# Moving the work tiles of an attention and MLP kernel by 32 bytes in SBUF, relative to the weights

## The chip, the cores and the metric

One core of one Trainium2 chip runs the whole program. The metric is the time of one execution in device microseconds; the time of a kernel is the median of its runs.

## What is computed

Attention with 4 sink positions and a sliding window of 128, over 4 batches of 8 heads of 768 tokens with head size 64, and then a two-layer MLP on the 3072 resulting rows.

```python
scores = scale * np.matmul(q, k.transpose(0, 1, 3, 2))
keep = is_sink | in_window
scores = np.where(keep, scores, -1000000000.0)
a = np.exp(scores - max); a = a / (np.sum(a, axis=-1, keepdims=True) + 1e-09)
x = np.matmul(a, v)            # heads side by side: (3072, 512)
h = x @ w_in                   # (512, 2048)
g = h * erf(softplus(h))
return g @ w_out               # (2048, 512)
```

## The kernel before

The MLP works on 12 groups of 256 tokens. For each group it goes over 16 blocks of 128 hidden columns (`hidden`, L524 to L535), and multiplies each pair of blocks with the second weights (`project`, L560 to L573). Attention for the next group is computed in between, in 48 steps of two heads each (`load`, `prep`, `core`, `norm`, `ptrans`, `av`, `xfin`), placed by a table `plan` and by priorities.

Apart from the first group, both products are made from values split in two parts of type float32r. The weights lie as `wt` tiles of two parts; the tokens as `xh` and `xl` (written in `xfin`); the hidden values as `g` with two parts (written in `act`). Three products of parts make one product:

- L533, `h<-xh,wt` and `h<-xl,wt`: a slice of `wt` of 128 x 128 is loaded into TensorE (PEld), then 256 columns of `xh` or `xl` are streamed through it (PE). 12 such pairs make one block of one group; 2112 in all.
- L570, `o<-wt,g`: 128 x 128 of `g` are loaded, then 512 columns of `wt` are streamed. 1056 in all.

So `x` streams against loaded `wt`, and `wt` streams against loaded `g`. While one matmul streams, the weight load of the next one runs. In the first group the same two products are made in plain fp32 instead (L529 and L570 with `wf`, `xf` and `gf`), as two passes of the matmul.

SBUF is given out by pools, one after another, in the order in which the pools are opened: `wpool` (33 tiles of 4096 bytes in each partition), then `pers` (`tri`, `kq`, `sv`, `pst`, two `sh` tiles and a tile `gap` that nothing reads or writes), then `raw` (the loaded `q`, `k`, `v`) and `work` (`u`, `pt`, `uo`, `sp`, `xh`, `xl`, `r`, `g`, `acc`). All `wpool` tiles have the same rest modulo 256, since 4096 is a multiple of 256; call it W. The tiles of `pers` take 64 + 11520 + 2048 + 4608 + 896 + 896 bytes, and `gap` another 128, together 20160 = 78 x 256 + 192. So `raw` and `work` begin at W + 192, that is 64 bytes below W modulo 256; every tile in them is a multiple of 256 bytes long, and so they all begin there. `kq`, `sv` and `pst` begin at W + 64, and `sh` at W + 64 and W + 192.

```python
shs = [pers.tile([P, 7, 2 * SW], F32R, name=f"sh{i}") for i in range(2)]
for x in shs:
    nc.gpsimd.memset(x[:, 6].bitcast(F32), 0.0)
pers.tile([P, 32], F32, name="gap")
```

With "distance" this document means the address of the operand that is being loaded as weights minus that of the operand that is being streamed at that time, modulo 256. Within L533 it is +64 before the change, and within L570 it is -64. At the change from a run of L533 to one of L570 (`g` loaded while `x` streams) it is 0, and so it is from L570 to L533.

Of the kernel before, what the change touches and what calls it, by code (L numbers as in the profile page):

```python
# [9 lines left out]
F32 = mybir.dt.float32  # L10
# [9 lines left out]
P = 128  # L20
# [30 lines left out]
def kernel(  # L51
# [77 lines left out]
    def fast_path():  # L129
        with ExitStack() as st:  # L130
            pers = st.enter_context(tc.tile_pool(name="pers", bufs=1))
# [44 lines left out]
            shs = [pers.tile([P, 7, 2 * SW], F32R, name=f"sh{i}") for i in range(2)]  # L176
            for x in shs:
                nc.gpsimd.memset(x[:, 6].bitcast(F32), 0.0)
            pers.tile([P, 32], F32, name="gap")
            xp = {}  # L180

            stp = {}
# [397 lines left out]
    def general_path():  # L580

        NT_S = S // P
        with ExitStack() as st:
# [71 lines left out]
            with tc.tile_pool(name="g_one1", bufs=1) as one, tc.tile_pool(name="g_work1", bufs=2) as work:  # L655
# [3 lines left out]
                with tc.For_i(0, B, 1) as b:  # L659
                    for gb in range(GPB):  # L660
# [25 lines left out]
                        for i in range(2):  # L686
# [3 lines left out]
                            )  # L690

    fast_path()
    ok = nc.values_load(flagi[0:1, 0:1], min_val=0, max_val=1)
    with tc.If(ok == 0):
# [31 lines left out]
```

## Time and profile before

| | |
|---|---|
| median of 3 runs | 765.98 us (763.82 to 767.38) |
| the profiled execution | 765.26 us |
| its span, first to last instruction | 763.3 us |
| TensorE matmul (PE) busy | 718.0 us, 94% |
| weight load (PEld) busy | 598.2 us, 78% |
| VectorE (DVE), ScalarE (ACT), GpSimd (POOL) busy | 69%, 70%, 27% |

Three views matter here. The busy time by stretch tells which engine is full, and at what clock. The groups by line tell how many matmuls there are of each kind; their mean is the length of one from its start to its end, which overlaps with the next one. The timeline merges equal instructions that follow each other, with the start of the first and a count: the start of a later row less that of an earlier one, divided by the number of matmuls between, is the time that one matmul takes of the engine, and is called its spacing here.

### The profile page before, as it was taken

Reading aid. Unit: us, or ns where it says so; the run is one execution under the profiler, and the core shown is the slowest. Engines: PE = TensorE matmul, PEld = TensorE weight load, DVE = VectorE, ACT = ScalarE, POOL = GpSimd, SP = SyncE. Lnnn points to the kernel's source line nnn. Section 1 sums busy time; section 2 is a strip of 40 time slices with the busy share of each in tenths; the row PEclk is TensorE's granted clock in tenths of the full one; section 3 lists DMA queues with packets and bytes.
Section 4 is the critical chain, followed back from the end, with each engine's and each line's share of the span. In section 5 each row is a group of like instructions: output and inputs, shape, how many; then the busy total and the mean of one; then the engine's idle time right before and its main releaser. Section 6 shows DMA issues by size and latency. Waiting matters only on the chain.

```text
span 763.3 us, 14942 instructions
## 1 busy us (share of the span) xinstructions
PE 718.0 (94%) x5168; PEld 598.2 (78%) x5168; DVE 526.5 (69%) x1509; ACT 535.0 (70%) x1261; POOL 202.6 (27%) x212
## 2 busy tenths in 40 slices
PE   2577998999999999999999999999999999999997
PEld 2345664887888898888888888888888888888885
DVE  6978998888676576576586586586576586584352
ACT  2356578897786687677787687687686687686473
POOL 1211220133322223232322232332322232322122
PEclk8679998999999999999999999999999999999999
DMA  6776530211211211211121211111111111100000
GB/s 203 218 231 198 218 86 15 76 23 26 61 44 31 67 45 25 63 31 32 56 49 30 59 42 37 55 41 29 56 38 42 56 46 36 39 12 1 28 1 32
DMA packets 100595, 47.33 MB, mean 62 GB/s; under 512 B 89248, under 2 KB 93344, under 8 KB 100512
## 3 DMA queue, kind: packets, MB, share of 16 engines
q1 hardware_dynamic: 100224, 46.29, 21.8%
q8 instruction: 43, 0.70, 0.4%
q14 instruction: 40, 0.33, 0.1%
q10 hardware_dynamic: 288, 0.00, 0.0%
HBM read 37.88 MB, written 6.29 MB: 58 GB/s over the span
## 4 chain that ended last, share of the span: by engine, by line
PE 76%; DVE 10%; ACT 6%; DMA 4%; issue 2%; SPq 1%; POOL 1%; ACTq 0%; DVEq 0%; POOLq 0%
PE o L570 30%; PE h L533 27%; PE av L361 5%; PE ps L272 4%; PE tqk L220 3%; PE tp L317 3%; PE h L529 2%; DVE pst L307 2%; DVE acc L552 1%; ACT u L550 1%; DMA ws<-in_moe_w_out_dram 1%; PE ts L338 1%; DVE w L442 1%; ACT pst L293 1%; DMA out_dram<-ot 1%
## 5 line engine op out<-in xcount | busy, mean ns | idle before, releaser
L570 PE MATMUL o<-wt,g 128*128 128x512 f32 x1056 | 270.0, 399 | 1.1 <-POOL g L558 0.5
L570 PEld LDWEIGHTS o<-wt,g 128*128 128x128 f32 x1056 | 189.0, 188 | 36.5 <-POOL g L558 1.3
L533 PE MATMUL h<-xh,wt 128*128 128x256 f32 x1408 | 203.7, 282 | 1.8 <-DVE acc L552 1.1
L533 PEld LDWEIGHTS h<-xh,wt 128*128 128x128 f32 x1408 | 184.7, 189 | 11.4 <-DVE acc L552 1.8
L558 POOL TENSOR_TENSOR g<-acc,g 128x512 fp32r<-128x512 f32 x88 | 114.7, 1303 | 291.7 <-DVE g L557 182.7
L550 ACT ACTIVATE u<-r 128x512 f32<-128x512 f32 x288 | 165.0, 623 | 13.5 <-DVE wf L448 4.4
L323 POOL TENSOR_SCALAR_AFFINE_SELECT uo<-pt 128x512 f32<-128x512 f32 (+1 forms) x96 | 83.1, 887 | 252.5 <-ACT pt L319 231.8
L552 DVE SCALAR_TENSOR_TENSOR acc<-u,acc 128x512 f32<-128x512 f32 x176 | 128.4, 730 | 19.1 <-ACT u L550 2.8
L552 DVE SCALAR_TENSOR_TENSOR acc<-u,h 128x512 f32<-128x512 f32 x88 | 60.4, 687 | 108.3 <-POOL g L558 60.3
L533 PE MATMUL h<-xl,wt 128*128 128x256 f32 x704 | 111.2, 279 | 0.0
L293 ACT ACTIVATE pst<-pst,kq 128x144 f32<-128x144 f32 x192 | 77.4, 405 | 25.7 <-DVE kq L289 24.6
L533 PEld LDWEIGHTS h<-xl,wt 128*128 128x128 f32 x704 | 94.2, 188 | 0.0
L545 ACT ACTIVATE r<-h 128x512 f32<-128x512 f32 x96 | 57.0, 593 | 25.8 <-PE h L533 24.9
L546 ACT ACTIVATE r<-r 128x512 f32<-128x512 f32 x96 | 61.1, 637 | 2.0
L547 ACT ACTIVATE r<-r 128x512 f32<-128x512 f32 x96 | 60.6, 631 | 2.6
L307 DVE TENSOR_SCALAR pst<-pst,kq 128x144 f32<-128x144 f32 x192 | 57.2, 360 | 1.5
L317 PE MATMUL tp<-ident,pst 128*128 128x128 f32 x192 | 36.4, 291 | 17.5 <-DVE pst L307 17.2
L557 DVE CAST g<-acc 128x512 fp32r<-128x512 f32 x88 | 44.3, 504 | 12.1 <-PE o L570 8.1
L223 ACT COPY kq<-tqk 128x512 f32<-128x512 f32 x48 | 28.0, 585 | 33.7 <-PE tqk L220 31.6
L361 PE MATMUL av<-uo,v 128*64 128x128 f32 (+1 forms) x512 | 50.1, 328 | 1.2 <-POOL uo L323 1.2
L377 ACT CAST xh<-av 128x256 fp32r<-128x256 f32 x44 | 16.0, 365 | 49.2 <-PE av L361 49.2
L272 PE MATMUL ps<-kq 64*64 64x208 f32 (+1 forms) x768 | 49.5, 369 | 0.0
(78 smaller groups left out, 723.0 us busy)
## 6 DMA issues: line engine op xcount, KB each, us to landing
ws<-in_moe_w_in_dram SPq DMA_DIRECT2D x16, 512.0 KB, 5.8
ws<-in_moe_w_out_dram SPq DMA_DIRECT2D x16, 512.0 KB, 5.0
q<-in_q_dram SPq DMA_DIRECT2D x96, 64.0 KB, 2.2
k<-in_k_dram SPq DMA_DIRECT2D x96, 64.0 KB, 2.2
v<-in_v_dram SPq DMA_DIRECT2D x64, 96.0 KB, 2.4
out_dram<-ot SPq DMA_DIRECT2D x24, 256.0 KB, 2.0
v<-in_v_dram SPq DMA_DIRECT2D x32, 64.0 KB, 2.2
kq<-kq SPq DMA_DIRECT2D x32, 64.0 KB, 2.0
```

The lines of the kernel that those rows point to most:

```text
L272: nc.tensor.matmul(ps[h][hf, x : x + n], qt[r, hf], kt[r, r0 : r0 + n], start=True, stop=True),
L293: nc.scalar.activation(y, y, AF.Exp, bias=d["neg"][:, i, h : h + 1], scale=-1.0, accum_out=d["sum"][:, i, h : h + 1])
L307: nc.vector.tensor_scalar_mul(p, p, sm[:, i, h : h + 1])
L323: nc.gpsimd.affine_select(out=uo[:, :, i1:, e, :], in_=pt[:, :, i1:, :], pattern=[[0, 2], [0, 2 - i1], [-sg, P]], compare_op=op, fill=0.0, ...
L361: prev, nc.tensor.matmul(o, x[:, h, :], y[:, h, :], start=False, stop=(m == len(ops) - 1), skip_group_check=True)
L533: nc.tensor.matmul(o, wt[NC * j + c][:, p, fs], xt[e][:, c, :], start=(m == 0), stop=(m == len(ops) - 1))
L546: nc.scalar.activation(r, r, AF.Square, bias=b_v, scale=-0.5)
L547: nc.scalar.activation(r, r, AF.Square, bias=b_r)
L550: nc.scalar.activation(u, r, AF.Square, bias=b_a[i], scale=CS)
L552: nc.vector.scalar_tensor_tensor(out=acc, in0=u, scalar=CC[i] * CS**2, in1=x, op0=ALU.add, op1=ALU.mult)
L558: nc.gpsimd.tensor_tensor(gl, acc, gh.bitcast(F32), op=ALU.subtract)
L570: nc.tensor.matmul(self.acc[g, i], gt[e][:, n0 : n0 + P], w, start=(f == 0 and m == 0), stop=(f == NF - 1 and m == len(ops) - 1),)
```

## The change

The unused tile `gap` grows from 32 to 40 floats, so every tile of `raw` and `work` moves up by 32 bytes in each partition. They begin 32 bytes below W modulo 256 now. The tiles of `wpool` and the other tiles of `pers` stay, and no instruction is added, removed or put elsewhere. The distance within L533 becomes +32, that within L570 -32; at the change from one to the other it stays 0.

```diff
             for x in shs:
                 nc.gpsimd.memset(x[:, 6].bitcast(F32), 0.0)
-            pers.tile([P, 32], F32, name="gap")
+            pers.tile([P, 40], F32, name="gap")
             xp = {}
```

## Rows read from the trace of the kernel before

**Rows 1.** The page, part 1: engine busy us (share of the span) and instructions.

```profile
PE 718.0 (94%) x5168; PEld 598.2 (78%) x5168; DVE 526.5 (69%) x1509; ACT 535.0 (70%) x1261; POOL 202.6 (27%) x212
```

**Rows 2.** Busy time by stretch: us, then each engine, clock, DMA share, GB/s.

```profile
0.00:50.00 50.00, 22.44 (x153) 14.64 (x153) 41.74 (x158) 17.33 (x60) 9.16 (x22) 0.75 0.75 226
50.00:100.00 50.00, 44.64 (x238) 31.29 (x236) 43.10 (x114) 28.89 (x71) 8.38 (x8) 0.94 0.62 200
...
200.00:300.00 100.00, 99.62 (x767) 85.95 (x767) 68.91 (x200) 77.01 (x180) 28.63 (x29) 1.00 0.19 47
...
600.00:700.00 100.00, 99.63 (x774) 86.64 (x772) 67.25 (x195) 75.91 (x176) 30.01 (x28) 1.00 0.13 34
700.00:763.30 63.30, 56.68 (x349) 49.57 (x345) 23.35 (x38) 34.50 (x59) 12.93 (x10) 1.00 0.05 19
```

**Rows 3.** Groups by line on PE: count, busy us, mean ns, idle before.

```profile
L570 PE MATMUL o<-wt,g 128*128 128x512 f32 x1056 | 270.0, 399 | 1.1 <-POOL g L558 0.5 <-ACT ot L577 0.4
L533 PE MATMUL h<-xh,wt 128*128 128x256 f32 x1408 | 203.7, 282 | 1.8 <-DVE acc L552 1.1 <-DVE gf L552 0.7
L533 PE MATMUL h<-xl,wt 128*128 128x256 f32 x704 | 111.2, 279 | 0.0
...
L529 PE MATMUL h<-xf,wf 128*128 128x256 f32 x128 | 31.5, 399 | 4.6 <-DVE gf L552 4.6
```

**Rows 4.** Timeline of PE, 196.6 to 201.2 us: start, length, instruction, count.

```profile
196.62 0.62 PE L570 MATMUL o<-wt,g 128*128 128x512 f32 x2
197.08 0.40 PE L533 MATMUL h<-xh,wt 128*128 128x256 f32 x2
197.31 0.63 PE L533 MATMUL h<-xl,wt 128*128 128x256 f32 x4
197.78 1.07 PE L533 MATMUL h<-xh,wt 128*128 128x256 f32 x8
198.69 0.62 PE L533 MATMUL h<-xl,wt 128*128 128x256 f32 x4
199.14 0.39 PE L533 MATMUL h<-xh,wt 128*128 128x256 f32 x2
199.37 0.62 PE L533 MATMUL h<-xl,wt 128*128 128x256 f32 x4
199.82 1.07 PE L533 MATMUL h<-xh,wt 128*128 128x256 f32 x8
200.73 0.62 PE L533 MATMUL h<-xl,wt 128*128 128x256 f32 x4
201.18 0.62 PE L570 MATMUL o<-wt,g 128*128 128x512 f32 x2
```

**Rows 5.** Timeline of PE, 670.6 to 674.2 us, same columns.

```profile
670.62 0.85 PE L570 MATMUL o<-wt,g 128*128 128x512 f32 x3
671.30 1.11 PE L533 MATMUL h<-xh,wt 128*128 128x256 f32 x8
672.25 0.63 PE L533 MATMUL h<-xl,wt 128*128 128x256 f32 x4
672.72 1.11 PE L533 MATMUL h<-xh,wt 128*128 128x256 f32 x8
673.66 0.64 PE L533 MATMUL h<-xl,wt 128*128 128x256 f32 x4
674.13 0.63 PE L570 MATMUL o<-wt,g 128*128 128x512 f32 x2
```

**Rows 6.** Timeline of PE, an L570 run of 17.

```profile
243.08 4.05 PE L570 MATMUL o<-wt,g 128*128 128x512 f32 x17
246.97 0.27 PE L317 MATMUL tp<-ident,pst 128*128 128x128 f32 x1
```

**Rows 7.** Timeline of PE, 81 to 88 us: the same lines in plain fp32.

```profile
81.29 3.60 PE L570 MATMUL o<-wf,gf 128*128 128x512 f32 x8
84.72 3.62 PE L529 MATMUL h<-xf,wf 128*128 128x256 f32 x16
```

**Rows 8.** Groups by line on PE, 197.67 to 201.18 us.

```profile
L533 PE MATMUL h<-xh,wt 128*128 128x256 f32 x18 | 2.5, 276 | 0.0
L533 PE MATMUL h<-xl,wt 128*128 128x256 f32 x15 | 2.4, 277 | 0.0
```

**Rows 9.** Groups by line on PE, 222.37 to 222.39 us.

```profile
L533 PE MATMUL h<-xh,wt 128*128 128x256 f32 x1 | 0.3, 279 | 0.0
L353 PE MATMUL av<-sp,sv 128*128 128x256 f32 x1 | 0.3, 277 | 0.0
```

**Rows 10.** The page, part 6: DMA issues, KB each, us to landing.

```profile
ws<-in_moe_w_in_dram SPq DMA_DIRECT2D x16, 512.0 KB, 5.8
...
q<-in_q_dram SPq DMA_DIRECT2D x96, 64.0 KB, 2.2
k<-in_k_dram SPq DMA_DIRECT2D x96, 64.0 KB, 2.2
...
out_dram<-ot SPq DMA_DIRECT2D x24, 256.0 KB, 2.0
```

**Rows 11.** Waits, 0 to 60 us: us in total, times, longest.

```profile
PE tqk L220 <- DMA k<-in_k_dram: 6.5, 1, 6.5
```

## The prediction, made before the changed kernel ran

> **What bounds the kernel now.** I read three views, in this order. The page's first part says that TensorE is the fullest engine: 718.0 us of a span of 763.3, while DVE and ACT stand near 70% [rows 1]. The busy time by stretch says where: from 200 to 700 us PE is busy 99.6 us of every 100, at the full clock of 2.4 GHz (1.00); only in the first 100 us, where the DMA share is 0.75 and 0.62, does it have real gaps [rows 2]. So for two thirds of the span a nanosecond more or less per matmul comes out at the end almost whole. The groups by line then say which matmuls: 2112 of L533 (1408 and 704) and 1056 of L570 [rows 3]. Nearly no idle time stands before them (1.1, 1.8 and 0.0 us), so their price is their spacing.
>
> The timeline gives the spacing, and shows that it isn't one number. In one run of L533, 30 matmuls from 197.78 to 201.18 us take 3.40 us, 113.3 ns each [rows 4]. In another run of the same line, same tiles, same clock, 24 matmuls from 671.30 to 674.13 take 2.83 us, 117.9 ns each [rows 5]. I call these the short and the long rhythm; they are 4.6 ns apart, and a row of matmuls of one line stays in one of them. The one of short rhythm begins with longer steps: its first 6 matmuls take 0.70 us, 116.7 each [rows 4]. An L570 run of 17 takes 3.89 us, 228.8 each [rows 6]. In the first group, plain fp32 streams the same columns in passes at half the rate: 8 of L570 in 3.43 us, 429 each, and 16 of L529 in 3.62 us with the last one's 0.40 in it, 215 each [rows 3, 7]. Half of those, 214 and 107, is what 512 and 256 columns would take if streaming were never held up. Float32r is 14 and 6 ns above that, so something holds the float32r streams up, and what differs between rhythms is a small hold of about 4.6 ns, present or absent.
>
> **Does the address matter?** The trace has other distances than +64 and -64 at the seams. At the end of that row of short rhythm the last L533 streams while `g` is loaded, at distance 0: the four matmuls before that seam take 0.45 us (200.73 to 201.18), as do four inside it (198.69 to 199.14) [rows 4]. So 0 costs no more than +64. The last L533 before L353 streams while `sv` is loaded, at distance +128: it lasts 279 ns where its like in the short rhythm lasts 276 [rows 8, 9]. L570 at the seams, with one distance of 0 each, shows 0.46 us for two (230 each) and 0.68 for three (227 each), on both sides of 228.8 [rows 4 to 6]. So distance +128 may cost some ns, and 0 and 64 can't be told apart.
>
> The Trainium skill (TensorE: Matmul & The Clock Gate, Part 2, step 1) says that weight load and streaming operand have SBUF read ports of their own, and that loading the next weights takes no read bandwidth from the running matmul. By that rule the two large terms below are exactly zero, with no range. The trace bears it out only in part: 279 against 276 at +128 [rows 8, 9] speaks against it, and two rhythms at the same addresses [rows 4, 5] it doesn't explain.
>
> **The change part by part.** No instruction is added, removed or moved, so only prices can change.
>
> 1. L533, distance +64 to +32: 2112 matmuls. How many run in which rhythm I can't count from grouped rows, so I take the middle, 115.6. All in the short rhythm would give -2.3 x 2112 = -4.9 us; all in the slow one +4.9; with no hold at all, at 107.3, -8.3 x 2112 = -17.5. I take 0: +32 lies between +64 and 0, and those two agree.
> 2. L570, distance -64 to -32: 1056 matmuls. With no hold, 214.4 instead of 228.8, -15.2 us; with one more hold of 4.6 each, +4.9. I take 0 by the same reason: -32 lies between -64 and 0.
> 3. Other matmuls whose operands move against each other are the transposes of `q` and `k` and the 48 of L353. At most one hold of 4.6 ns on some 250 matmuls is 1.1 us either way; I take 0.
> 4. DVE, ACT and POOL read and write moved tiles. ACT has 23 us free in each 100 and DVE 31 [rows 2], so a small change there is covered by PE; without that cover it would show on the chain, which I don't expect.
> 5. DMA: `q`, `k` and `v` now land 32 bytes past where they did, in pieces of 256 bytes. They take 2.2 us to land [rows 10], and from 200 us on the DMA share is under 0.2 [rows 2], so nothing waits. At the start PE waits once for `k`, 6.5 us [rows 11]; the bounds are 0 and a doubling of that, +6.5, and I take 0: it is one wait, and the other loads are issued well ahead of their use.
>
> The Trainium skill (DMA: Bandwidth & Descriptors, How a descriptor splits into AXI transactions) has a rule against this change: transactions start at multiples of 256 bytes and cost beats of 32, so a piece of 256 bytes that starts at a rest of 64 costs 10 beats, and at a rest of 96 it costs 11. If it holds on the SBUF side, my estimate by that page is a tenth of the 6.5 us, +0.65, and the sum would be +0.65 instead of 0. No row of this trace shows it.
>
> Sum: 0 us. Against the profiled execution's 765.26 that is 765.3; the median of the runs shown is 765.98, 0.7 above it, so in medians the forecast is **766.0**. Its own range is 762 to 770: about half a percent, 3.8 us, is what a measurement of this kernel can tell from no change, and I use that bound for all chances.
>
> **The rivals.**
>
> - *Long rhythm everywhere* (the other side). At +32 the load and the stream meet in a way that no distance of the trace shows, every run of L533 stays in the long rhythm (+4.9), and each L570 takes one more hold (+4.9): 766.0 + 9.8 = 775.8; with the first alone 770.9. It decides from a mean spacing of L533 about 1.8 ns higher, 3.8 us over 2112. For it: the long rhythm exists and is stable [rows 5]; the tiles now lie an odd multiple of 32 bytes from the weights, which no operand of these matmuls did. Against: 0 is as good as +64 in [rows 4]. Chance 0.28.
> - *Short rhythm everywhere.* At +32 the streams are farther from +128, the one distance with a visible price. The long starts and the long rhythm vanish: -4.9, 761.1; if one hold also leaves each L570, another -4.9, 756.2. If all holds left, 766.0 - 32.7 = 733; nothing in the trace shows a float32r run near that, so I give it 0.03 of the chance. For it: the short rhythm exists at the same clock [rows 4]. Against: PE may then start to wait for ACT, which has only 23 us free in 100 [rows 2]. Chance 0.32.
> - *The address plays no part at all*, and rhythms come from the order in which runs begin. Then the time is 766.0, as forecast; its chance is in the forecast's.
> - *The tiles don't really move.* Then nothing changes, either. The sizes of the tiles in that pool leave no room for it: 32 bytes are 32 bytes.
>
> **How the numbers follow.** The forecast, with the no-address case in it, has 0.40. Between it and the two rivals on either side no row decides; faster gets a little more than slower, since the known bad distance is +128 and both new distances are farther from it. The range takes the longer rival whole (775.8) and the shorter one down to 756.2, some of its own spread left out: 755 to 776. That leaves out about 0.1 to 0.15.
>
> **What would show it.** Right: L533 runs of the changed kernel still at 113.3 and 117.9 ns in a like mix, L570 runs at 228.8, PE busy near 718 us, and the same 6.5 us wait at the start. Wrong: a spacing that neither trace of before has (109, 111, 122 for L533; under 226 or over 233 for L570), or only one of the two rhythms left. If PE's spacing is unchanged and the time isn't, the first 100 us and the DMA landing times are where I would look.

## The result, and the profile after

The changed kernel takes 773.28 us (median of 4 runs, 772.12 to 774.12), the kernel before in the same comparison 766.16: a ratio of 1.0096, 95% interval 1.0068 to 1.0123. It is slower by about 7.1 us. That is inside the stated range of 755 to 776, but it is not the "no change" that was forecast.

The page of the changed kernel, part 1, against [rows 1]:

```profile
PE 727.7 (94%) x5168; PEld 604.0 (78%) x5168; DVE 524.6 (68%) x1509; ACT 536.1 (69%) x1261; POOL 201.5 (26%) x212
```

Only TensorE has more to do with the same 5168 matmuls and weight loads: PE 9.7 us more, PEld, which overlaps with PE, 5.8. DVE, ACT and POOL are within 2 us. The busy time by stretch, against [rows 2]:

```profile
0.00:50.00 50.00, 22.27 (x153) 14.57 (x153) 41.52 (x156) 17.35 (x59) 9.18 (x22) 0.76 0.76 225
50.00:100.00 50.00, 44.72 (x237) 31.20 (x235) 43.01 (x114) 28.95 (x70) 8.39 (x8) 0.94 0.63 201
...
200.00:300.00 100.00, 99.73 (x756) 85.61 (x755) 68.45 (x195) 76.04 (x175) 28.40 (x29) 1.00 0.18 45
```

The first 100 us are as before. In the stretch from 200 to 300 us PE is as full as it was and its clock is 1.00 as it was, but it gets through 756 matmuls where there were 767. So the time went into the single matmul, not into waits. The groups by line, against [rows 3], say into which:

```profile
L570 PE MATMUL o<-wt,g 128*128 128x512 f32 x1056 | 272.9, 401 | 1.1 <-POOL g L558 0.5 <-ACT ot L577 0.4
L533 PE MATMUL h<-xh,wt 128*128 128x256 f32 x1408 | 207.5, 284 | 1.5 <-DVE acc L552 0.8 <-DVE gf L552 0.7
L533 PE MATMUL h<-xl,wt 128*128 128x256 f32 x704 | 113.6, 282 | 0.0
```

L533 is busy 6.2 us longer and L570 2.9; together that is 9.1 of the 9.7. The timeline of the same row of 36 matmuls of L533 that stands in [rows 4]:

```profile
197.41 0.40 PE L533 MATMUL h<-xh,wt 128*128 128x256 f32 x2
197.65 0.64 PE L533 MATMUL h<-xl,wt 128*128 128x256 f32 x4
198.12 1.11 PE L533 MATMUL h<-xh,wt 128*128 128x256 f32 x8
199.07 0.63 PE L533 MATMUL h<-xl,wt 128*128 128x256 f32 x4
...
200.25 1.11 PE L533 MATMUL h<-xh,wt 128*128 128x256 f32 x8
201.20 0.63 PE L533 MATMUL h<-xl,wt 128*128 128x256 f32 x4
201.67 0.40 PE L570 MATMUL o<-wt,g 128*128 128x512 f32 x1
```

36 matmuls from 197.41 to 201.67 take 4.26 us, 118.3 ns each; before, the same 36 took 4.10 us (197.08 to 201.18), 113.9. The start times of the single matmuls show this in every one of the 95 rows of twelve or more: past its first steps each has a mean of 117.0 to 119.2 ns, also the one of [rows 5], which was in the long rhythm. And the L570 row of [rows 6]:

```profile
244.09 4.13 PE L570 MATMUL o<-wt,g 128*128 128x512 f32 x17
248.05 0.27 PE L317 MATMUL tp<-ident,pst 128*128 128x128 f32 x1
```

17 in 3.96 us are 232.9 each, where it was 228.8. From the start times of all matmuls in the traces, over all pairs of neighbours of one line that follow each other without a break (1913 pairs of L533, 854 and 855 of L570), the **mean spacing** goes from 115.1 to 118.3 ns for L533 and from 229.6 to 232.9 for L570. Times the counts of [rows 3] that is 2112 x 3.2 + 1056 x 3.3 = 10.2 us. That takes the matmuls at the seams to have grown as much as their neighbours inside. PE's busy time grew by 9.7, and its idle time fell from 45.3 to 44.4, so the span of the profiled execution grew by 8.8 (763.3 to 772.1). The medians are only 7.1 apart because the execution profiled before lay 0.9 below the median of its kernel and the one after 0.8 above. The loads of `q` and `k` didn't change. Part 6 of the page, and the wait of PE in the first 60 us:

```profile
q<-in_q_dram SPq DMA_DIRECT2D x96, 64.0 KB, 2.2
k<-in_k_dram SPq DMA_DIRECT2D x96, 64.0 KB, 2.2
```

```profile
PE tqk L220 <- DMA k<-in_k_dram: 6.5, 1, 6.5
```

### The profile page after: what moved, and what is told of

Its sections match the earlier page's. It is cut to its first block, busy times and chain, and to the rows that moved or that the text cites. A ratio compares the mean times of both kernels' runs of the same rounds, so it can differ in the third digit from the quotient of the medians.

```text
span 772.1 us, 14942 instructions
## 1 busy us (share of the span) xinstructions
PE 727.7 (94%) x5168; PEld 604.0 (78%) x5168; DVE 524.6 (68%) x1509; ACT 536.1 (69%) x1261; POOL 201.5 (26%) x212
## 4 chain that ended last, share of the span: by engine, by line
PE 79%; DVE 10%; DMA 4%; ACT 3%; issue 1%; SPq 1%; POOL 1%; ACTq 0%; DVEq 0%; POOLq 0%
PE o L570 31%; PE h L533 29%; PE av L361 5%; PE ps L272 5%; PE tqk L220 3%; PE tp L317 3%; PE h L529 2%; DVE w L442 1%; DVE pst L307 1%; DVE wf L448 1%; DVE acc L552 1%; PE ts L338 1%; DMA out_dram<-ot 1%; DVE w L439 1%; ACT pst L293 1%
## 5 line engine op out<-in xcount | busy, mean ns | idle before, releaser
L570 PE MATMUL o<-wt,g 128*128 128x512 f32 x1056 | 272.9, 401 | 1.1 <-POOL g L558 0.5
L570 PEld LDWEIGHTS o<-wt,g 128*128 128x128 f32 x1056 | 188.9, 188 | 39.3 <-POOL g L558 1.3
L533 PE MATMUL h<-xh,wt 128*128 128x256 f32 x1408 | 207.5, 284 | 1.5 <-DVE acc L552 0.8
L533 PEld LDWEIGHTS h<-xh,wt 128*128 128x128 f32 x1408 | 187.4, 188 | 11.5 <-DVE acc L552 1.5
L533 PE MATMUL h<-xl,wt 128*128 128x256 f32 x704 | 113.6, 282 | 0.0
L533 PEld LDWEIGHTS h<-xl,wt 128*128 128x128 f32 x704 | 96.2, 189 | 0.0
```

Of the source, the lines that this page charges most:

```text
L533: nc.tensor.matmul(o, wt[NC * j + c][:, p, fs], xt[e][:, c, :], start=(m == 0), stop=(m == len(ops) - 1))
L570: nc.tensor.matmul(self.acc[g, i], gt[e][:, n0 : n0 + P], w, start=(f == 0 and m == 0), stop=(f == NF - 1 and m == len(ops) - 1),)
```

## The experiments

In all of them the instructions of every engine stand in the order of before; only addresses differ. In all but one `x` and `g` get pools of their own, and unused pads set where each pool begins. Each kernel has one trace, so a mean spacing is that of one execution; the ratios are from several.

**Which tiles?** Theory A says the distance of each line sets that line's price; B blames the loads and the other engines' tiles; C says that both lines must move together. First `x` alone (`xf` and `gf` of the first group move with `x` and `g`; their lines and those that hand the pools on are left out):

```diff
 work = st.enter_context(tc.tile_pool(name="work", bufs=2))
+gp_ = st.enter_context(tc.tile_pool(name="gpool", bufs=2))
+padx = st.enter_context(tc.tile_pool(name="padx", bufs=1)); padx.tile([P, 8], F32, name="padx")
+xp_ = st.enter_context(tc.tile_pool(name="xpool", bufs=2))
...
-xp[g] = [work.tile([P, NC, GT], F32R, tag="x" + t, name=f"x{t}_{g}") for t in "hl"]
+xp[g] = [xp_.tile([P, NC, GT], F32R, tag="x" + t, name=f"x{t}_{g}") for t in "hl"]
...
-gt = work.tile([P, 2, 512], F32R, tag="g", bufs=2, name=f"g_{m}")
+gt = self.gp.tile([P, 2, 512], F32R, tag="g", bufs=2, name=f"g_{m}")
```

> Only xh, xl (and xf) lie 32 bytes below the weights' rest; g and all other work tiles stay 64 below. Theory A (the distance between the operand being loaded and the one being streamed sets the price of a matmul, each line for itself): L533 goes from a mean near 115 ns to near 118 ns as in the changed kernel, 2112 x 3.2 = +6 to +7 us, L570 stays near 229.5; the time is about 772, ratio 1.006 to 1.009. Theory B (the loads of q, k, v or the other engines' tiles cost the time): no change, 766. Theory C (the two lines disturb each other, and only both together give the loss): +0 to +3 us.

Measured: 771.26 us, ratio 1.0062 (1.0040 to 1.0084). Mean spacing 118.2 for L533 and 229.5 for L570: the one has the whole change, the other none of it. For `g` alone the pad stands ahead of the pool of `g`, behind that of `x`:

> Only g lies 32 bytes below the weights' rest; x and all other work tiles stay 64 below. Theory A: L570 goes from about 229.5 to about 233 ns, 1056 x 3.3 = +3.5 us, L533 keeps its two rhythms of 113.3 and 117.8; the time is about 769, ratio 1.003 to 1.005. Theory B: no change, 766. Theory C: +0 to +3 us, with L533 changed as well.

Measured: 771.35 us, ratio 1.0069 (1.0044 to 1.0094). L570 has 233.2, as theory A foretold, but its time, about 769 (ratio 1.003 to 1.005), lies below what was measured. L533 was to keep its two rhythms, and does, but not their shares: its mean is 116.6. The row of [rows 4], in short rhythm before, is now in the long one:

```profile
197.09 0.40 PE L533 MATMUL h<-xh,wt 128*128 128x256 f32 x2
197.32 0.64 PE L533 MATMUL h<-xl,wt 128*128 128x256 f32 x4
...
200.86 0.64 PE L533 MATMUL h<-xl,wt 128*128 128x256 f32 x4
201.33 0.86 PE L570 MATMUL o<-wt,g 128*128 128x512 f32 x3
```

36 in 4.24 us, 117.8 each, although neither `x` nor the weights moved. By spacing the two halves therefore add up to more than the whole: 6.5 us for `x` alone (2112 x 3.1) and 7.0 for `g` alone (2112 x 1.5 + 1056 x 3.6) against 10.2. With `x` at 32 below there is no short rhythm left to lose. The times, 0.62% and 0.69% against 0.96%, point the same way, but their intervals are too wide to show it. For the rest of the tiles the pools of `x` and `g` come first, and the pad of 32 bytes stands between them and `raw`:

> x and g stay 64 bytes below the weights' rest; q, k, v and the other work tiles (u, pt, uo, sp, r, acc) lie 32 below. Theory A: no change, 766 within half a per cent, L533 and L570 as before. Theory B: the whole loss, about 773, with later loads of q, k, v or longer instructions on DVE, ACT or POOL. Theory C: no change.

Measured: 767.19 us, ratio 1.0009 (0.9994 to 1.0025), L533 115.7, L570 230.1. Theories B and C fall: B had the whole loss here, and C at most 3 us for one line alone. A stands, with the addition that L533's rhythm also depends on where other tiles lie. These other tiles, too, put some rows of L533 into the long rhythm (115.7 against 115.1); what that costs, 1.3 us by the spacing of L533, is inside the interval.

**Is it the distance, or the place?** Here a pad of 32 bytes stands ahead of the weights, so that weights, `x`, `g` and everything behind them lie 32 further on together; the constants ahead of the pad, `ident` among them, stay.

```diff
 mask0 = cpool.tile([P, KB], BF16, name="mask0")
+cpool.tile([P, 8], F32, name="shift")
```

> The weights and everything behind them move up by 32 bytes together, so that all distances are those of before, while every address lies where the changed kernel has x and g. If the distance counts (theory A): 766, L533 near 115, L570 near 229.5. If it is the place of x and g itself that counts (an odd multiple of 32 as a start address): near 773, L533 near 118, L570 near 233.

Measured: 765.85 us, ratio 0.9997 (0.9981 to 1.0012), L533 115.2, L570 229.6. The row of 36:

```profile
198.12 0.40 PE L533 MATMUL h<-xh,wt 128*128 128x256 f32 x2
...
201.78 0.62 PE L533 MATMUL h<-xl,wt 128*128 128x256 f32 x4
202.23 1.08 PE L570 MATMUL o<-wt,g 128*128 128x512 f32 x4
```

4.11 us, 114.2 each, with `x` at the very rest modulo 256 at which the changed kernel has it. So the start address itself doesn't set the price. With the runs above, it is the distance to the weights.

**Which distances are dear?** The other six multiples of 32, with `x` and `g` moved together and the other tiles left at 64 below. For level and 32 above a pad stands ahead of the two pools, behind `work`. For the other four the two pools come ahead of `raw`, `gap` has another size, and a second pad brings `raw` and `work` back to their place. The edit for `x` and `g` at the weights' own rest:

```diff
+padx = st.enter_context(tc.tile_pool(name="padx", bufs=1)); padx.tile([P, 16], F32, name="padx")
+xp_ = st.enter_context(tc.tile_pool(name="xpool", bufs=2)); gp_ = st.enter_context(tc.tile_pool(name="gpool", bufs=2))
```

> x and g begin at the weights' rest itself, so the distance is 0 within L533 and within L570. Theory D (a distance that is an odd multiple of 32 is dear, multiples of 64 are cheap): L533 keeps rhythms near 113.3 and 117.8, mean near 115, L570 near 229 to 231; the time is 764 to 768. Theory E (the price rises as the two addresses come closer than 64): 0 is worse than 32, L533 over 118.3 and L570 over 233, the time over 775.

> x and g begin 64 bytes above the weights' rest: distance -64 within L533, +64 within L570, the signs of before exchanged. Theory D: like before, L533 near 115, L570 near 229 to 231, 764 to 768. Theory E: like before as well, if only nearness counts. If the sign counts, L533 or L570 changes by over 2 ns.

> x and g begin 96 bytes below the weights' rest: distance +96 within L533, -96 within L570. Theory D: as dear as the changed kernel, L533 near 118.3, L570 near 233, time near 773. Theory E: farther apart than before, so no dearer than before: at most 766.

> x and g begin 128 bytes from the weights' rest, as far as can be. Theory D: cheap like other multiples of 64, about 766, unless the 2 to 3 ns seen in the trace of before at +128 hold for all 2112 and 1056 matmuls: then L533 near 118 and up to +6 us. Theory E: the cheapest of all, under 766.

> x and g 32 bytes above the weights' rest: distance -32 within L533, +32 within L570. Each of the six places tried so far has a price of its own in each line, and only 64 below gave the short rhythm of 113.3 ns. Theory G (the price is a pattern of the distance with one good place): L533 between 117 and 120, L570 between 229 and 234, 769 to 776. Theory H (there is a second good place): L533 under 115 or L570 under 229, under 764.

> x and g 96 bytes above the weights' rest: distance -96 within L533, +96 within L570. Theory G: L533 between 117 and 120, L570 between 229 and 234, 769 to 776. Theory H: L533 under 115 or L570 under 229, under 764.

| `x` and `g`, from the weights' rest | L533, mean ns | L570, mean ns | ratio to before (95% interval) |
|---|---|---|---|
| 96 below | 118.2 | 233.4 | 1.0100 (1.0080 to 1.0119) |
| **64 below (before)** | **115.1** | **229.6** | 1 |
| 32 below (the change) | 118.3 | 232.9 | 1.0096 (1.0068 to 1.0123) |
| level | 119.5 | 229.7 | 1.0067 (1.0050 to 1.0084) |
| 32 above | 116.9 | 232.9 | 1.0061 (1.0038 to 1.0084) |
| 64 above | 117.7 | 233.3 | 1.0075 (1.0051 to 1.0099) |
| 96 above | 119.7 | 233.6 | 1.0130 (1.0101 to 1.0159) |
| 128 off | 119.0 | 231.3 | 1.0102 (1.0082 to 1.0122) |

D (odd multiples of 32 are dear) falls: level and 64 above are multiples of 64, and L533 is dear in both. E (nearness is dear) falls: 96 and 128 off are dear too, and level is cheap for L570. The sign counts: 64 below and 64 above differ by 2.6 and 3.7 ns. H falls: at neither of its two places is L533 under 115 or L570 under 229. G is near but missed twice by a little, with 116.9 for L533 at 32 above (117 to 120 was expected) and 776.8 us at 96 above (769 to 776). What is left is the table: each distance has its price in each line, and of the eight only 64 below is cheap in both. Since `g` alone also changes the mean of L533, a mean of L533 in the table isn't the price of its own distance alone. In the level kernel the row of [rows 4] reads

```profile
197.67 0.40 PE L533 MATMUL h<-xh,wt 128*128 128x256 f32 x2
...
201.51 0.64 PE L533 MATMUL h<-xl,wt 128*128 128x256 f32 x4
201.99 0.63 PE L570 MATMUL o<-wt,g 128*128 128x512 f32 x2
```

which is 4.32 us for 36, 120.0 each. Distance 0 was one of the two that I had taken for the ends of an interpolation, and as a steady row it is the dearer one.

**A better mix?** The last kernel combines the best place of each line, `x` 64 below and `g` level.

> x stays 64 bytes below the weights' rest and g begins at it: distance +64 within L533, 0 within L570. These are the best places that the runs so far show for each line (115.1 and 229.7 ns, the latter as good as 229.6 at 64 below). Theory A alone: like before, 765 to 768, L533 near 115, L570 near 229.7. Theory I (the rhythm of a row of L533 is set by how the L570 ahead of it left off): the share of L533 in the long rhythm changes with g although x stays; all short would be 113.4 and 762, all long 117.8 and 771.

Measured: 766.79 us, ratio 1.0021 (1.0010 to 1.0033); no gain. L570 is a little better than it ever was, 228.6, but L533 has 116.3. Two rows of the same 36 matmuls in this one kernel, near 198 and near 313 us:

```profile
197.68 0.40 PE L533 MATMUL h<-xh,wt 128*128 128x256 f32 x2
...
201.79 0.63 PE L570 MATMUL o<-wt,g 128*128 128x512 f32 x2
```

```profile
312.63 0.40 PE L533 MATMUL h<-xh,wt 128*128 128x256 f32 x2
...
316.88 0.61 PE L570 MATMUL o<-wt,g 128*128 128x512 f32 x2
```

4.11 us (114.2 each) and 4.25 us (118.1): both rhythms again, with the long one now the commoner. The sum by lines, 2112 x 1.2 - 1056 x 1.0 = +1.5 us, is the measured +1.54 (766.79 less 765.25). So which rhythm a row of L533 gets changes with `g` alone. Theory I says more, that what stands ahead of a row sets its rhythm, and the start times bear that out. Of the 95 rows of L533 with twelve matmuls or more, 64 follow L570 with `wt` and `g`, and 31 another matmul, in 30 cases one of the attention. The table counts those in the short rhythm, by the mean step past the first six and without the last two; it is under 115.3 in them and over 117 in all others.

| kernel | short, behind L570 | short, behind another matmul |
|---|---|---|
| before | 54 of 64 | 25 of 31 |
| weights and all behind them moved | 54 of 64 | 25 of 31 |
| `g` alone, 32 below | 7 of 64 | 22 of 31 |
| `x` 64 below, `g` level | 8 of 64 | 27 of 31 |
| the other tiles alone, 32 below | 53 of 64 | 9 of 31 |

Moving `g` turns the rows behind L570 and hardly the others. Moving the attention's tiles turns those behind attention: behind the transposes of `q`, 14 of 15 rows are short before and 1 of 15 with `q` moved. Where all distances to the weights are those of before, the counts are the same. Whether L570 does it by its own distance or by that at the seam, where `g` is loaded while `x` streams and which moved as well, isn't separated. No version tried beats the kernel before.

## Why the prediction was right and where it was wrong

- **The number:** inside the range, but not by the forecast. 773.28 lies 7.3 us above 766.0 and outside the forecast's own 762 to 770; the range holds it because it took in the rival of 770.9 to 775.8.
- **That only prices can change, and on TensorE:** right. PE's idle time went from 45.3 to 44.4 us, and from 200 to 300 us PE is 99.7% busy.
- **Terms 1 and 2, L533 and L570 at 0:** wrong, and this is the step that failed. "+32 lies between +64 and 0, and those two agree" rested on single matmuls at the seams, where distance 0 had cost nothing. One matmul at another distance at the end of a row of the old distance doesn't show what a whole row of it costs: at distance 0 L533 takes 119.5 on average, 4.4 more than at +64. The step at the seam goes with its row: at the same distance 0 between `g` and `x` it takes 114.6 ns before and 119.8 in the level kernel (means of some 75 seams). And there is no "between": the price isn't smooth in the distance, as the table shows. The terms measured +6.8 us (2112 x 3.2) and +3.5 us (1056 x 3.3). The second is inside its bound of +4.9. The first is outside: the bound took L533 from 115.6 to 117.9, and it went from 115.1 to 118.3.
- **The rival "long rhythm everywhere":** right in sign, place and size (770.9 to 775.8; it is 773.3), not in detail. The rows don't fall into the old long rhythm, whose steps are 117 to 119, but into a pattern of their own with steps of 115 to 123 and 118.3 on average. Its chance of 0.28 was low against 0.40 for a forecast that had only the seams behind it.
- **The rival "short rhythm everywhere", at 0.32:** wrong in sign; no row in short rhythm is left. What it had against +128 did hold, though on one matmul's 3 ns: a whole kernel at 128 off has L533 at 119.0.
- **The address plays no part:** wrong. The rule of the Trainium skill (TensorE: Matmul & The Clock Gate, Part 2, step 1), that loading the next weights takes no read bandwidth from the running matmul, would give the same spacing for every row of the table, as the prediction used it; the measured means go from 115.1 to 119.7 and from 229.6 to 233.6, and the measurement decides. That reads collide isn't shown by this.
- **Terms 3 to 5:** right; the run with only the other tiles moved stays within 0.25%. The rule of the Trainium skill on 256-byte transactions (DMA: Bandwidth & Descriptors, How a descriptor splits into AXI transactions) would, if it held on the SBUF side, have made the pieces dearer; 2.2 us to land and a wait of 6.5 us are what they were.
- **The signs of being wrong** that were named: the one on rhythms came, as no row in short rhythm is left; L570, at 232.9, stayed just under its sign of 233.

What stays open: what in SBUF or TensorE makes a pair of addresses dear. The runs show that it is the distance between `wt` and the other operand, line by line, at one clock and beside the same other work; that the load of the next weights and the running stream hinder each other is the reading that fits, but no run took the loads away. The records of single weight loads don't show it either: those of L533 are 188.5 ns long on average before and after. Steps finer than 32 bytes, and whether the pattern repeats every 256, weren't tried.

## What to carry to other kernels

In a kernel like this one, where TensorE is full and streams float32r, the addresses of its two operands relative to each other were worth 0.6 to 1.3%, and a pad of a few floats decides it. Try the places on the chip, since neither nearness nor alignment to 64 foretold the price. Don't move such tiles by accident: a tile added between them and the weights does it when its size isn't a multiple of 256 bytes. And don't price a steady state by single events at its seams.

## What was not expected of the hardware

- The same matmul on the same addresses has several stable rhythms (113.3 and 117.9 ns for 256 columns), and which one a row gets depends on the matmuls ahead of it: with only `g` moved, a row of L533 went from 113.9 to 117.8, and of the 64 rows behind L570 those in short rhythm went from 54 to 7.
- Plain fp32 passes at half the rate show no such effect: with `xf` and `gf` at all eight places, their mean spacing stays between 215.9 and 216.1 ns for 256 columns and between 429.3 and 430.1 for 512.
- The best of the eight places was the one that the kernel had; the worst, 96 above, costs 1.3%.
